# Routed experts' first product as Strassen's seven block products over 256 of 384 rows

## The chip, the core and the metric

The kernel runs on one core of a Trainium2 chip. The metric is the device time of one execution in microseconds (us); the time of a version is the median of its runs. The engines are TensorE (PE in the rows, PEld for its weight loads), VectorE (DVE), ScalarE (ACT), GpSimd (POOL) and SyncE (SP, which issues DMAs). Each engine works through its own queue in order; an instruction that waits holds up all that stand behind it on its engine.

## The reference, cut

The program is an attention-like recurrence, a dense feed-forward layer ("m" below) and a layer of eight routed experts ("e"). The change touches the experts:

```python
def _moe2_ref(x, w_gate, w1, w2):        # x: 1536 x 384, w1: 8 x 384 x 1024, w2: 8 x 1024 x 384
    P = ...                              # 1536 x 8 gate, eight Sinkhorn rounds over x @ w_gate
    out = np.zeros((N, D), dtype=np.float32)
    for e in range(E):
        h = np.maximum(x @ w1[e], 0.0)
        ye = h @ w2[e]
        out += P[:, e:e + 1] * ye
    return out
```

All products have fp32 inputs. The kernel splits every operand into a high and a low part (`hi` is a copy rounded to fp32r, `lo` the remainder), and forms each product as three matmuls: hi·hi, hi·lo, lo·hi.

## The kernel before

There are three stages on PE: the attention front with the first part of the dense layer (0 to about 100 us), the dense layer with the rest of the attention in between (to about 314 us), and the experts (from about 311 to 1119 us). This document is about the last.

The 1536 tokens are three blocks `tb` of 512, the 1024 hidden units of an expert eight blocks `f` of 128. A step is one (e, tb, f): `e_l1` (L652) makes the first product, three `d` blocks of 128 rows with three matmuls each, nine matmuls of 512 columns into bank 0 or 1 (L658 to L660); ScalarE takes the ReLU into `hh` (L663), VectorE the remainder into `hl` (L664). `e_l2` (L667) makes the second product of the step two before: for four groups `j` of 128 tokens three matmuls of 384 columns into banks 2 to 5 (L675 to L677), which add up over the eight `f`. After `f` = 7 VectorE adds the four banks times the gate to `acc` (L688), and for the last expert SyncE stores them.

Weights come as pieces of 128x768 (`setup_weights`, L61): four "a" pieces (w1) and four "b" pieces (w2) an expert. `split_pieces` (L100) loads a piece by SyncE into one of two `raw` buffers of two pieces each, makes `hi` on ScalarE (L113) and `lo` on GpSimd (L114).

From expert 4 on, `w_range` (L693) reads inputs again to test their range: three tiles of 128x1536 with two reductions each (L702, L703), then sixteen of 128x768 with one ScalarE and three VectorE instructions each (L718 to L722). Its tiles take turns with the weight pieces in the `raw` buffers. The order of all this within each engine's queue is set by a scheduler that follows the order of the code, the buffers and its own model of times.

## Time and profile before

| | us |
|---|---|
| median of 3 runs | 1129.66 (1129.65 to 1129.84) |
| profiled execution, device time | 1127.9 |
| its span, first to last instruction | 1126.0 |
| PE busy | 1103.7, 98% |
| DVE / ACT / POOL busy | 477.6 / 322.5 / 151.2 |
| granted TensorE clock, mean | 0.993 |

A matmul's time in the rows is from its start to its modelled end, and the next one starts before that end: what a matmul costs PE is the distance of starts. For the other engines the time of a row is the time of the instruction.

### The profile page before, as it was taken

To read this page: it belongs to the slowest core of one execution; us is meant where nothing else is said; L and a number is where in the kernel's file an instruction comes from. 1 tells how busy PE (TensorE), PEld (TensorE's weight loads), DVE (VectorE), ACT (ScalarE), POOL (GpSimd) and SP (SyncE) were. 2 spreads that over 40 slices of the span, in tenths; PEclk is the share of its full clock that TensorE was granted. 3 is DMA by queue.
4 is the path that set the end of the run, shared out by engine and by line. 5 is a ranking of instruction groups with operands and counts; after the bars stand their busy time and mean duration, and the time that the engine had idled before them with its cause. 6 is when DMAs were issued, how large, how long until landed. Compare 5 with 4: busy or idle time off the path is not lost.

```text
span 1126.0 us, 17562 instructions
## 1 busy us (share of the span) xinstructions
PE 1103.7 (98%) x7376; PEld 995.3 (88%) x7376; DVE 477.6 (42%) x873; ACT 322.5 (29%) x615; POOL 151.2 (13%) x129
## 2 busy tenths in 40 slices
PE   8799999999999999999999999999999999999997
PEld 7677899999989999999999999899999989999996
DVE  7899777774334211222222422562354232122221
ACT  3445344435632441122113112321331231111110
POOL 1002011101710130031003001300210130000000
PEclk9899999999999999999999999999999999999999
DMA  7556212100510021012002200530252020000000
GB/s 207 163 182 199 96 56 71 57 17 5 169 57 1 1 84 29 1 32 81 1 1 84 84 1 30 173 118 19 84 178 76 4 82 1 1 1 1 29 29 31
DMA packets 26920, 71.26 MB, mean 63 GB/s; under 512 B 4128, under 2 KB 11280, under 8 KB 26832
## 3 DMA queue, kind: packets, MB, share of 16 engines
q1 hardware_dynamic: 24528, 57.46, 16.3%
q0 software_dynamic: 2304, 12.58, 3.5%
...
HBM read 65.31 MB, written 2.36 MB: 60 GB/s over the span
## 4 chain that ended last, share of the span: by engine, by line
PE 89%; DMA 4%; issue 2%; DVE 2%; POOL 1%; ACT 1%; SPq 0%; DVEq 0%; POOLq 0%; ACTq 0%
PE bank L675 12%; PE bank L677 11%; PE bank L676 11%; PE bank L659 11%; PE bank L660 11%; PE bank L658 11%; PE bank L583 3%; PE bank L585 3%; PE bank L584 3%; PE bank L564 3%; PE bank L566 3%; PE bank L565 3%; DMA raw<-in_moe_w_in_dram 1%; DMA wh<-in_moe_w_in_dram 1%; DMA lv<-in_vn_dram 1%
## 5 line engine op out<-in xcount | busy, mean ns | idle before, releaser
L664 DVE SCALAR_TENSOR_TENSOR hl<-bank,hh 128x512 fp32r<-128x512 f32 x192 | 132.1, 689 | 434.4 <-ACT hh L663 434.1
L675 PE MATMUL bank<-whi,hh 128*128 128x384 f32 x768 | 259.0, 337 | 0.7 <-ACT hh L663 0.7
L676 PE MATMUL bank<-wlo,hh 128*128 128x384 f32 x768 | 258.3, 336 | 0.0
L677 PE MATMUL bank<-whi,hl 128*128 128x384 f32 x768 | 254.2, 337 | 0.0
L663 ACT ACTIVATE hh<-bank 128x512 fp32r<-128x512 f32 x192 | 114.4, 596 | 488.1 <-PE bank L660 477.3
L660 PE MATMUL bank<-x2h,wlo 128*128 128x512 f32 x576 | 227.9, 396 | 0.0
L659 PE MATMUL bank<-x2l,whi 128*128 128x512 f32 x576 | 227.5, 395 | 0.0
L658 PE MATMUL bank<-x2h,whi 128*128 128x512 f32 x576 | 224.5, 390 | 0.0
L114 POOL TENSOR_TENSOR wlo<-raw,whi 128x768 fp32r<-128x768 f32 x64 | 118.2, 1857 | 564.8 <-ACT whi L113 546.8
L675 PEld LDWEIGHTS bank<-whi,hh 128*128 128x128 f32 x768 | 144.3, 188 | 9.6 <-ACT hh L663 1.1
L676 PEld LDWEIGHTS bank<-wlo,hh 128*128 128x128 f32 x768 | 144.2, 188 | 7.9 <-issue 0.2
L677 PEld LDWEIGHTS bank<-whi,hl 128*128 128x128 f32 x768 | 143.9, 188 | 2.4
L660 PEld LDWEIGHTS bank<-x2h,wlo 128*128 128x128 f32 x576 | 108.0, 187 | 22.3
L658 PEld LDWEIGHTS bank<-x2h,whi 128*128 128x128 f32 x576 | 108.2, 188 | 17.2 <-issue 0.2
L659 PEld LDWEIGHTS bank<-x2l,whi 128*128 128x128 f32 x576 | 108.0, 188 | 17.2
L564 PE MATMUL bank<-x1h,whi 128*128 128x256 f32 (+1 forms) x240 | 75.6, 316 | 5.3 <-ACT x1h L448 2.3
L113 ACT CAST whi<-raw 128x768 fp32r<-128x768 f32 x64 | 53.3, 837 | 95.0 <-PE bank L659 40.9
L565 PE MATMUL bank<-x1l,whi 128*128 128x256 f32 (+1 forms) x240 | 74.6, 312 | 0.6 <-DVE x1l L453 0.6
L688 DVE SCALAR_TENSOR_TENSOR acc<-bank,P,acc 128x384 f32<-128x384 f32 x84 | 48.0, 611 | 63.3 <-PE bank L677 63.3
L583 PE MATMUL bank<-gh,whi 128*128 128x256 f32 (+1 forms) x240 | 74.5, 316 | 0.0
L566 PE MATMUL bank<-x1h,wlo 128*128 128x256 f32 (+1 forms) x240 | 74.3, 311 | 0.0
L584 PE MATMUL bank<-gl,whi 128*128 128x256 f32 (+1 forms) x240 | 73.2, 306 | 0.0
...
## 6 DMA issues: line engine op xcount, KB each, us to landing
...
```

The lines of the kernel that those rows point to most:

```text
L114: (nc.vector if i < N64 else nc.gpsimd).tensor_sub(lo, raw, hi.bitcast(F32))
L564: nc.tensor.matmul(ps, lhsT=wh, rhs=xh[:, d, :], start=(d == 0), stop=False)
L565: nc.tensor.matmul(ps, lhsT=wh, rhs=xl[:, d, :], start=False, stop=False)
L583: nc.tensor.matmul(ps, lhsT=wdh, rhs=gh, start=first, stop=False)
L658: nc.tensor.matmul(ps, lhsT=wh, rhs=xh[:, d, :], start=(d == 0), stop=False)
L659: nc.tensor.matmul(ps, lhsT=wh, rhs=xl[:, d, :], start=False, stop=False)
L660: nc.tensor.matmul(ps, lhsT=wl, rhs=xh[:, d, :], start=False, stop=(d == 2))
L663: nc.scalar.activation(hh, ps, ACTF.Relu)
L664: nc.vector.scalar_tensor_tensor(hl, ps, 0.0, hh.bitcast(F32), op0=ALU.max, op1=ALU.subtract)
L675: nc.tensor.matmul(ps, lhsT=hh[:, sl], rhs=wh, start=st, stop=False)
L676: nc.tensor.matmul(ps, lhsT=hh[:, sl], rhs=wl, start=False, stop=False)
L677: nc.tensor.matmul(ps, lhsT=hl[:, sl], rhs=wh, start=False, stop=sp)
```

## The change

The first product over the first two of the three `d` blocks (256 of 384 rows) is made for two `f` blocks at once by the Winograd form of Strassen's scheme. A pair is one (e, tb, p) with p = 0 to 3, the blocks f = 2p and 2p+1; there are 96 pairs, twelve an expert. The 256 rows by 256 hidden units by 512 tokens are a 2x2 by 2x2 block product with blocks of 128x128 and 128x256. `e_step` forms seven block products (21 matmuls of 256 columns) in place of eight of twice three matmuls, and the third `d` block as before (`e0`, `e1` with `d2`: six matmuls of 512 columns). The block sums of the tokens are made in `split_x2`, once per `tb` (VectorE); those of the weights, s1 to s4, in `split_pair`, once per "a" piece (GpSimd), which stores nine blocks of 128 in place of six. The sums of the products are made in each pair: two ScalarE copies out of PSUM, four VectorE additions of 256 columns, two of 512 columns that join them with the bank; ReLU and remainder then read the result `sums` in SBUF, no longer the bank.

The second product's instructions are the same, but come as eight parts a pair (one per `f` and `j`) from a list `todo`, which `e_step` draws on between its products: 2, 2, 1 and the rest. The PSUM banks of a pair, A (first `f`), B (second `f`) and C (the products s1·t1 and, one after the other, a11·b11, s2·t2, s3·t3) come from a ring of banks 0, 1, 6 and 7. The pieces of an expert are loaded b first, then a, at places in `split_e`; `w_range` moves two steps per pair, as before two steps per two `f`. The logits, the x2 split of the last block and the Sinkhorn rounds are written after the first pair. The dense layer's "a" weights are stored in tiles of 1152 instead of 768 columns; three of its pieces are split by two instructions instead of one.

The diff, cut to its core:

```diff
-K = {'tk': (4, 0, 2, 4, 6), 'wr': (4, 0), 'wm': 1, 'gate': (0, 2)}
+K = {'ring': 6, 'tk': (4, 0, 2, 4, 6), 'wr': (4, 0), 'wm': 1, 'gate': (0, 2)}
+    def split_pair(self, e, p, raw):
+        a11, a12, a22, _, _, a21 = (raw[:, j * 128:(j + 1) * 128] for j in range(6))
+        t = self.t_p.tile([128, 512], F32, tag="t", name="ws")
+        s1, s2, s3, s4 = (t[:, j * 128:(j + 1) * 128] for j in range(4))
+        nc.gpsimd.tensor_add(s1, a21, a22)
+        nc.gpsimd.tensor_sub(s3, a11, a21)
+        nc.gpsimd.tensor_sub(s2, s1, a11)
+        nc.gpsimd.tensor_sub(s4, a12, s2)
+        hi, lo = self.wt[e, p, "a"] = self.w_tiles()
+        for src, sl in ((raw[:, 0:640], slice(0, 640)), (t, slice(640, 1152))):
+            nc.scalar.copy(hi[:, sl], src)
+            nc.gpsimd.tensor_sub(lo[:, sl], src, hi[:, sl].bitcast(F32))
...
     def split_x2(self, tb):
+        nc.vector.tensor_sub(t1, b12, b11)
+        nc.vector.tensor_sub(t3, b22, b12)
+        nc.vector.tensor_sub(t2, b22, t1)
+        nc.vector.tensor_sub(t4, b21, t2)
+        for src, j, o in ((b11, 0, 0), (x[:, 1, :], 0, 256), (ta, 0, 768), (t3, 0, 1280), (t4, 1, 0), (x[:, 2, :], 1, 256)):
+            nc.scalar.copy(hl[0][j][:, sl], src)
+            nc.vector.tensor_sub(hl[1][j][:, sl], src, hl[0][j][:, sl].bitcast(F32))
...
-    def e_l1(self, i, e, tb, f):
+    def e_banks(self, n):
+        if n < K['ring']:
+            c, a = (7, 0) if n % 2 == 0 else (0, 7)
+            return [self.banks[j] for j in (a, 1, c)]
+        ring = self.ring = [1, 0, 7, 6] if n == K['ring'] else [self.ring[j] for j in (3, 0, 1, 2)]
+        return [self.banks[ring[j]] for j in (1, 2, 0)]
+    def e_step(self, n, e, tb, p, fill):
+        def mm(ps, w, x, start=False, stop=False):
+            nc.tensor.matmul(ps, lhsT=uh, rhs=xh, start=start, stop=False)
+            nc.tensor.matmul(ps, lhsT=uh, rhs=xl, start=False, stop=False)
+            nc.tensor.matmul(ps, lhsT=ul, rhs=xh, start=False, stop=stop)
+        def relu(f, ps, sums):
+            nc.vector.tensor_add(sums, ps, sums)
+            nc.scalar.activation(hh, sums, ACTF.Relu)
+            nc.vector.scalar_tensor_tensor(hl, sums, 0.0, hh.bitcast(F32), op0=ALU.max, op1=ALU.subtract)
+        mm(C1, "s1", "t1", start=True, stop=True)
+        mm(C0, "a11", "b11", start=True, stop=True)
+        nc.scalar.copy(sa[:, 0:256], C0)
+        nc.scalar.copy(p5, C1)
+        fill(2)
+        mm(A, "e0", "d2", start=True)
+        mm(A0, "a12", "b21")
+        mm(C0, "s2", "t2", start=True, stop=True)
+        nc.vector.tensor_add(u2, C0, sa[:, 0:256])
+        nc.vector.tensor_add(sa[:, 256:512], u2, p5)
+        fill(2)
+        mm(A1, "s4", "b22", stop=True)
+        relu(2 * p, A, sa)
+        mm(C0, "s3", "t3", start=True, stop=True)
+        nc.vector.tensor_add(sb[:, 0:256], C0, u2)
+        nc.vector.tensor_add(sb[:, 256:512], sb[:, 0:256], p5)
+        fill(1)
+        mm(Bk, "e1", "d2", start=True)
+        mm(B0, "a22", "t4", stop=True)
+        relu(2 * p + 1, Bk, sb)
+        fill(8)
...
-            self.wa_p = pool("wa", 8)
+            self.wa_p = pool("wa", 5)
...
+            split_e = (0, 1, 2, 2, 3, 4, 4, 5, 5, 6, 7, 8)
+            for n, (e, tb, p) in enumerate((e, tb, p) for e in range(E) for tb in range(3) for p in range(4)):
+                self.e_step(n, e, tb, p, fill)
+                if n == 0:
+                    self.logits(2)
+                    self.split_x2(2)
+                    self.sinkhorn()
+                todo += [lambda e=e, tb=tb, f=f, j=j: self.e_l2(e, tb, f, j) for f in (2 * p, 2 * p + 1) for j in range(4)]
+                self.split_pieces(N64 + 8 * (e + 1) + split_e[n % 12])
+                if not gen and (e, tb) >= K['wr']:
+                    next(wr, None)
+                    next(wr, None)
+            fill(8)
```

In the changed file the products of `mm` are at L730 to L732, `relu` at L737 to L739, the ScalarE copies at L746 and L747, the four additions at L752, L753, L758 and L759, the second product at L773 to L775, the sum into `acc` at L786, the reductions of `w_range` at L800 and L801 (wide tiles) and L817 to L820 (narrow), a piece's sums and `lo` at L174 to L177 and L181 (a) and L130 (b).

PE's queue in the middle of the experts. Before, three of the nine first products of a step end and the second products of another follow (`x2h`, `x2l` are tokens; `whi`, `wlo` weights):

```order
L658 MATMUL bank0_61<-x2h1_3804,whi_5256 128x512
L659 MATMUL bank0_61<-x2l1_3805,whi_5256 128x512
L660 MATMUL bank0_61<-x2h1_3804,wlo_5257 128x512
L675 MATMUL bank2_63<-whi_5176,hh_5722 128x384
L676 MATMUL bank2_63<-wlo_5177,hh_5722 128x384
L677 MATMUL bank2_63<-whi_5176,hl_5723 128x384
L675 MATMUL bank3_64<-whi_5176,hh_5722 128x384
```

Now, in pair 31 (banks A, B, C are 1, 0, 6): the last second products of pair 30, one product of pair 32's C, s3·t3 of pair 31 into bank 6, and pair 32's B into bank 1, which was pair 31's A:

```order
L774 MATMUL bank5_66<-wlo_5517,hh_6591 128x384
L775 MATMUL bank5_66<-whi_5516,hl_6592 128x384
L732 MATMUL bank7_68<-x2h_4171,wlo_5746 128x256
L730 MATMUL bank6_67<-x2h1_3838,whi_6071 128x256
L731 MATMUL bank6_67<-x2l1_3839,whi_6071 128x256
L732 MATMUL bank6_67<-x2h1_3838,wlo_6072 128x256
L730 MATMUL bank1_62<-x2h_4172,whi_5745 128x512
L731 MATMUL bank1_62<-x2l_4174,whi_5745 128x512
L732 MATMUL bank1_62<-x2h_4172,wlo_5746 128x512
L730 MATMUL bank1_62<-x2h_4172,whi_5745 128x256
L731 MATMUL bank1_62<-x2l_4174,whi_5745 128x256
L732 MATMUL bank1_62<-x2h_4172,wlo_5746 128x256
```

A pair's products are spread over its neighbours, and most of them stand in blocks of three of 256 columns.

VectorE's queue where the first two tiles of `w_range` are reduced (`wt`). Before:

```order
L688 SCALAR_TENSOR_TENSOR acc_4819<-bank4_65,P_72,acc_4819 128x384
L688 SCALAR_TENSOR_TENSOR acc_4819<-bank5_66,P_72,acc_4819 128x384
L664 SCALAR_TENSOR_TENSOR hl_6159<-bank0_61,hh_6158 128x512
L702 TENSOR_REDUCE wmm_6835<-wt_6836 128x1
L703 TENSOR_REDUCE wmm_6835<-wt_6836 128x1
L664 SCALAR_TENSOR_TENSOR hl_6189<-bank1_62,hh_6188 128x512
L664 SCALAR_TENSOR_TENSOR hl_6214<-bank0_61,hh_6213 128x512
L702 TENSOR_REDUCE wmm_6835<-wt_6890 128x1
L703 TENSOR_REDUCE wmm_6835<-wt_6890 128x1
L664 SCALAR_TENSOR_TENSOR hl_6239<-bank1_62,hh_6238 128x512
```

Now, from the first addition of pair 47 to the last before pair 48's first (banks A, B, C of pair 47 are 1, 0, 6):

```order
L752 TENSOR_TENSOR u2_7868<-bank6_67,esa_7869 128x256
L753 TENSOR_TENSOR esa_7869<-u2_7868,p5_7867 128x256
L800 TENSOR_REDUCE wmm_8025<-wt_8026 128x1
L801 TENSOR_REDUCE wmm_8025<-wt_8026 128x1
L737 TENSOR_TENSOR esa_7869<-bank1_62,esa_7869 128x512
L758 TENSOR_TENSOR esb_7870<-bank6_67,u2_7868 128x256
L759 TENSOR_TENSOR esb_7870<-esb_7870,p5_7867 128x256
L739 SCALAR_TENSOR_TENSOR hl_7906<-esa_7869,hh_7905 128x512
L737 TENSOR_TENSOR esb_7870<-bank0_61,esb_7870 128x512
L800 TENSOR_REDUCE wmm_8025<-wt_8107 128x1
L739 SCALAR_TENSOR_TENSOR hl_7925<-esb_7870,hh_7924 128x512
L801 TENSOR_REDUCE wmm_8025<-wt_8107 128x1
```

A pair has eight instructions of its own there; before, two steps had two. Both pairs of reductions stand in one pair's stretch. In pair 48's stretch, which follows, stand its eight, four L786, the third L800 and L801, six small ones, and one each of L817, L819 and L820.

GpSimd's queue in the experts. Before, one instruction a piece:

```order
L114 TENSOR_TENSOR wlo_5257<-raw_5099,whi_5256 128x768
L114 TENSOR_TENSOR wlo_5177<-raw_4934,whi_5176 128x768
L114 TENSOR_TENSOR wlo_5422<-raw_5260,whi_5421 128x768
L114 TENSOR_TENSOR wlo_5342<-raw_5099,whi_5341 128x768
L114 TENSOR_TENSOR wlo_5507<-raw_5260,whi_5506 128x768
```

Now (`ws` is s1 to s4): the last sums of three "a" pieces, the `lo` of two of them, and of two "b" pieces:

```order
L177 TENSOR_TENSOR ws_5041<-raw_4805,ws_5041 128x128
L177 TENSOR_TENSOR ws_5125<-raw_4805,ws_5125 128x128
L181 TENSOR_TENSOR wlo_4964<-raw_4574,whi_4963 128x640
L181 TENSOR_TENSOR wlo_4964<-ws_4958,whi_4963 128x512
L130 TENSOR_TENSOR wlo_5289<-raw_5052,whi_5288 128x768
L181 TENSOR_TENSOR wlo_5047<-raw_4805,whi_5046 128x640
L181 TENSOR_TENSOR wlo_5047<-ws_5041,whi_5046 128x512
L130 TENSOR_TENSOR wlo_5366<-raw_5052,whi_5365 128x768
```

An "a" and a "b" piece alternate, about one of each a pair, from pair 8 of an expert on, when the first weight buffers come free.

## Rows read from the trace of the kernel before

**Rows 1.** The page: busy time, share of the span, instructions.

```profile
PE 1103.7 (98%) x7376; PEld 995.3 (88%) x7376; DVE 477.6 (42%) x873; ACT 322.5 (29%) x615; POOL 151.2 (13%) x129
```

**Rows 2.** Windows, two stretches of experts: length, busy us by engine, clock, DMA share, GB/s.

```profile
450.00:700.00 250.00, 250.00 (x1257) 226.58 (x1256) 64.89 (x96) 50.50 (x79) 34.98 (x19) 1.00 0.11 33
700.00:900.00 200.00, 199.28 (x1000) 180.17 (x999) 88.14 (x123) 53.51 (x79) 29.36 (x16) 1.00 0.29 94
```

**Rows 3.** Timeline, PE, one step of the experts: start, us, instruction.

```profile
501.92 0.39 PE L658 MATMUL bank<-x2h,whi 128*128 128x512 f32 x1
...
504.00 0.33 PE L675 MATMUL bank<-whi,hh 128*128 128x384 f32 x1
...
506.11 0.39 PE L658 MATMUL bank<-x2h,whi 128*128 128x512 f32 x1
```

**Rows 4.** Timeline, PE, end of the dense layer: nine matmuls of 256 columns.

```profile
309.89 0.28 PE L583 MATMUL bank<-gh,whi 128*128 128x256 f32 x1
...
310.96 0.40 PE L658 MATMUL bank<-x2h,whi 128*128 128x512 f32 x1
```

**Rows 5.** Groups by line and shape: busy us, mean ns, idle before and releaser.

```profile
L675 PEld LDWEIGHTS bank<-whi,hh 128*128 128x128 f32 x768 | 144.3, 188 | 9.6 <-ACT hh L663 1.1 <-issue 0.2
L664 DVE SCALAR_TENSOR_TENSOR hl<-bank,hh 128x512 fp32r<-128x512 f32 x192 | 132.1, 689 | 434.4 <-ACT hh L663 434.1
L114 POOL TENSOR_TENSOR wlo<-raw,whi 128x768 fp32r<-128x768 f32 x64 | 118.2, 1857 | 564.8 <-ACT whi L113 546.8 <-issue 17.7
L663 ACT ACTIVATE hh<-bank 128x512 fp32r<-128x512 f32 x192 | 114.4, 596 | 488.1 <-PE bank L660 477.3 <-PE bank L676 10.5
L688 DVE SCALAR_TENSOR_TENSOR acc<-bank,P,acc 128x384 f32<-128x384 f32 x84 | 48.0, 611 | 63.3 <-PE bank L677 63.3
L719 DVE SCALAR_TENSOR_TENSOR wh<-wh 128x768 f32<-128x768 f32 x16 | 15.3, 957 | 34.2 <-ACT wh L718 34.2
L721 DVE TENSOR_REDUCE whm<-wh 128x1 f32<-128x768 f32 x16 | 15.1, 946 | 0.2
L343 POOL TENSOR_TENSOR kz<-at,zf 112x256 f32<-112x256 f32 x12 | 8.9, 745 | 69.2 <-issue 67.5 <-PE bank L237 1.6
L453 DVE TENSOR_TENSOR x1l<-x,x1h 128x256 fp32r<-128x256 f32 x18 | 7.3, 421 | 7.5 <-ACT x1h L448 4.7 <-DMA lv<-in_vn_dram 2.5
L702 DVE TENSOR_REDUCE wmm<-wt 128x1 f32<-128x1536 f32 x3 | 5.3, 1753 | 11.1 <-DMA wt<-in_w_dram 11.1
L251 DVE TENSOR_TENSOR x<-bank,cst 128x256 f32<-128x256 f32 x8 | 3.3, 416 | 0.1
```

**Rows 6.** One line's instructions (L572: 270 to 311 us): min/median/max ns, starts, shapes.

```profile
L664 DVE SCALAR_TENSOR_TENSOR hl<-bank,hh x192: 676/691/694, 310.7 to 1113.1; 128x512 fp32r<-128x512 f32 x192
L572 DVE TENSOR_TENSOR gl<-g,gh x17: 409/475/1874, 271.1 to 307.6; 128x256 fp32r<-128x256 f32 x17
```

**Rows 7.** Timeline, DVE and POOL, at 291 and at 584 us.

```profile
291.29 1.84 POOL L114 TENSOR_TENSOR wlo<-raw,whi 128x768 fp32r<-128x768 f32 x1
291.96 1.45 DVE L572 TENSOR_TENSOR gl<-g,gh 128x256 fp32r<-128x256 f32 x1 [2.37 <-ACT gh L571]
...
584.46 1.85 POOL L114 TENSOR_TENSOR wlo<-raw,whi 128x768 fp32r<-128x768 f32 x1 [62.78 <-ACT whi L113]
585.33 0.68 DVE L664 SCALAR_TENSOR_TENSOR hl<-bank,hh 128x512 fp32r<-128x512 f32 x1
```

**Rows 8.** Waits: engine, tile, line, releaser: us in total, times, longest.

```profile
ACT wh L718 <- DMA wh<-in_moe_w_in_dram: 24.4, 8, 5.9
DVE wmm L702 <- DMA wt<-in_w_dram: 11.1, 3, 4.0
```

**Rows 9.** Windows, the front: PE with gaps, and the clock after them.

```profile
40.00:44.00 4.00, 1.57 (x25) 0.99 (x22) 3.02 (x4) 1.92 (x4) 0.68 (x2) 1.00 0.92 278
44.00:48.00 4.00, 1.66 (x4) 1.12 (x5) 1.50 (x3) 0.41 (x1) 0.00 (x0) 0.67 0.66 237
48.00:52.00 4.00, 4.00 (x11) 3.02 (x11) 2.97 (x6) 0.93 (x2) 0.00 (x0) 0.50 0.00 1
```

**Rows 10.** Timeline, the end: the last matmul and the last sums into acc.

```profile
1117.55 2.19 DVE L688 SCALAR_TENSOR_TENSOR acc<-bank,P,acc 128x384 f32<-128x384 f32 x4 [3.73 <-PE bank L677]
...
1118.39 0.34 PE L677 MATMUL bank<-whi,hl 128*128 128x384 f32 x1
```

More of the change, by code (lines that the diff above doesn't have):

```diff
@@ L599, in logits @@
         nc = self.nc
-        ps = self.bank_y[:, 0:128]
+        ps = self.bank_u[:, 0:128]
         for d in range(3):
@@ new lines, in e_l2 @@
+        ps = self.banks[2 + j][:, 0:DM]
+        sl = slice(j * 128, (j + 1) * 128)
+        nc.tensor.matmul(ps, lhsT=hh[:, sl], rhs=wh, start=st, stop=False)
+        nc.tensor.matmul(ps, lhsT=hh[:, sl], rhs=wl, start=False, stop=False)
+        nc.tensor.matmul(ps, lhsT=hl[:, sl], rhs=wh, start=False, stop=sp)
+        if sp:
+            n = tb * 4 + j
+            g = self.P[:, n, e:e + 1]
+            if j == 0 and e == 0:
+                self.acc[tb] = self.x2_p.tile([128, 4, DM], F32, tag=f"x2_{tb}", name="acc")
+            acc = self.acc[tb][:, j, :]
+            if e == 0:
+                nc.scalar.copy(acc, ps)
+                nc.scalar.activation(acc, acc, ACTF.Copy, scale=g)
+            else:
+                nc.vector.scalar_tensor_tensor(acc, ps, g, acc, op0=ALU.mult, op1=ALU.add)
+            if e == E - 1:
+                nc.sync.dma_start(out=self.out[n * 128:(n + 1) * 128, :], in_=acc)
@@ new lines, in run, with fill @@
+            todo = [lambda s=s: self.m_l2(*s[1:]) for s in steps[-2:]]
+            def fill(k):
+                for _ in range(min(k, len(todo))):
+                    todo.pop(0)()
+            split_e = (0, 1, 2, 2, 3, 4, 4, 5, 5, 6, 7, 8)
[8 more added lines that the diff above has]
+                if not gen and (e, tb) >= K['wr']:
+                    if wr is None:
+                        wr = self.w_range()
+                    next(wr, None)
+                    next(wr, None)
```

195 lines of the change are left out of this document (95 added, 100 removed).

## The prediction

> **What bounds the kernel now.** I read the busy times first: PE is busy 98% of the span, every other engine under half [rows 1]. The windows say that this holds in the stage that changes: from 450 to 700 us PE is busy 250.00 of 250 us, from 700 to 900 it misses 0.7 us [rows 2]. So the experts are paced by PE's own work, and a saving there counts in full, as long as nothing that PE waits for becomes late. The timeline gives the price of a matmul: nine of 512 columns take from 501.92 to 504.00, 0.231 us each, twelve of 384 take 2.11 us, 0.176 each [rows 3]. Nine of 256 columns in a row, each with its own weight load, take 1.07 us, 0.119 each [rows 4]. Price goes with columns, plus some 0.013 us.
>
> **What PE saves.** Per pair the first product had 18 x 0.231 = 4.16 us. Now it has 21 x 0.119 + 6 x 0.231 = 2.50 + 1.39 = 3.89. The second product keeps 24 x 0.176 = 4.22. A pair falls from 8.38 to 8.11 us, and 96 pairs give 26.4 us. The rest of the change can only take from that.
>
> One rule of the Trainium skill speaks against this price. "TensorE: Matmul & The Clock Gate", section "Back-to-back issue gap", says that a stream of weight loads and matmuls is spaced by both together, about 81 ns at 128 columns and 131 at 512; between these 256 would be about 98 ns (estimate from that page), and the pair would cost 21 x 0.098 + 6 x 0.131 = 2.84 against 18 x 0.131 = 2.36 before, a loss of 46 us in all. The trace differs, with 231 ns at 512 and 119 at 256 [rows 3, 4], and the measurement decides.
>
> **What the other engines get.** Per pair VectorE had two instructions of 0.69 us [rows 5]. Now it has four additions of 256 columns (0.42 each: the nearest rows are L251, one input in PSUM, and L453, both in SBUF), two of 512 and two remainders of 512 (0.69 each): 4.44 us of 8.11. With the four sums into acc (0.61 each, every fourth pair) it is 6.9. ScalarE has two ReLUs of 0.60 and two copies that are no longer than these: under 2.4. On averages neither is the bound. What decides is lateness, and I followed PE's new order for it. After s2·t2 of a pair PE has twelve second products, s3·t3 and a few of 256 columns before the next pair's B takes over this pair's bank A: 2.5 to 3.2 us. In that time VectorE must do the first two additions and the one that empties A: 0.2 (drain of the last product) + 0.42 + 0.42 + 0.69 = 1.75. So 0.7 to 1.4 us are to spare; the other deadlines (ReLU, remainder, the addition that empties C) have 1 to 3. In an ordinary pair PE waits for nothing, and I price it at zero.
>
> **GpSimd bursts: 4 us.** What is new in kind is that four of VectorE's eight instructions read both inputs from SBUF, the remainder among them (before, one input was a PSUM bank). In the trace such an instruction is held up while GpSimd works: a subtraction of 0.41 us that starts inside a GpSimd one takes 1.45 and ends with it, while the remainder out of PSUM takes 0.68 beside GpSimd as always [rows 7]; over all starts the first form ranges from 0.41 to 1.87 us, the second from 0.68 to 0.69 [rows 6].
>
> The Trainium skill has this as a rule ("SBUF — State Buffer", section "Who interferes with whom"): a VectorE instruction with two SBUF inputs and a GpSimd instruction that reads SBUF exclude each other for a whole instruction. The trace agrees for VectorE [rows 6, 7]; by the rule GpSimd would be held up as well, which delays weights that are needed pairs later, and leaves my sum as it is.
>
> GpSimd's work grows. From 0.75 us at 256 columns and 1.86 at 768 [rows 5], an estimate by the straight line is 0.47 at 128, 1.30 at 512, 1.58 at 640. An "a" piece costs 4 x 0.47 + 1.30 + 1.58 = 4.8 (was 1.86), and from pair 8 of an expert on one "a" and one "b" piece go through per pair: 6.6 of 8.1 us for some five pairs, in seven experts. An instruction that comes at a random time waits for half the sum of squares over the pair: (4 x 0.22 + 1.69 + 2.50 + 3.46) / 16.2 = 0.53, less the 0.13 that overlap, 0.4 us. Four of them are 1.6 us, 4.44 becomes 6.0, still inside 8.1: free. Where the sums into acc fall into a burst (pairs 8 and 12) it is 6.9 + 1.6 = 8.5, and the spare of 0.7 to 1.4 is overrun by some 0.3. Price 14 x 0.3 = 4 us; bounds 0 and, with all of 1.6 us exposed in 35 pairs, 56. I stay near the low end, since the deadlines cover most of it.
>
> **The range test: 11 us.** `w_range` has the same work as before, but VectorE has less room. Around its start the order puts two tiles of 1.75 + 1.74 us [rows 5] into pair 47 and, into pair 48, another, four sums into acc, the first narrow tile (0.96 + 2 x 0.95) and small ones. Pair 47 has 4.44 + 7.0 = 11.4 us, pair 48 4.44 + 2.44 + 3.5 + 2.85 + 0.8 = 14.0: together 25.4 us of work in 16.2 us of PE's. No order inside the two pairs helps. Walking through: in pair 47 the first tile stands ahead of the addition that empties A, which ends at 5.2 instead of 1.75 us, and PE's 2.5 us of cover leave 2.8 of waiting; in pair 48 PE waits 0.5 for a remainder, 3.1 for the emptying of B behind the third tile, 1.0 for the next u2. That is 7.4, I take 7. The pairs from 57 to 63 and 69 to 73 have a narrow tile most times: 4.44 + 2.85 = 7.3, with acc 9.7, and they meet the burst's 1.6. Over 57 to 63 the order holds about 57 us of VectorE work, +6 of burst against 56.8 of PE, and over 69 to 73 about 39 + 6 against 40.5; less the spare, 3 us in the two. One us more for the loads: before, VectorE waited 3.7 us for each of three wide tiles and ScalarE 24 us in eight waits for narrow ones [rows 8], at no cost to PE; now a load that is late holds up additions that stand behind it. Sum 11, bounds 4 and 20.
>
> **Start and end: 4 us.** At pair 0 no second products are there to fill, and the split of the last x2 block shares VectorE: ahead of the addition that frees bank C stand five of 0.42 and one of 0.69, 2.8 us, against some 1.3 us of PE's work (s3·t3 and the logits); ahead of the first remainder another 4.4 us against 3.5. That is 1.5 + 0.9, plus one hold-up by GpSimd: 3 (1 to 6). At the end, after the last s3·t3, 0.2 + 0.42 + 0.42 + 0.69 + 0.60 + small waits = 2.5 lead to the last ReLU, against twelve second products, 2.1: 0.4; and the last four banks end 0.18 apart instead of 0.53, so that three more acc sums of 0.53 trail the last matmul, where it was one and a half [rows 10]: 0.8. Together 1.
>
> **At nothing.** The Strassen sums of the first two x2 blocks, the b-first loads and the moved splits lie under PE's dense layer; the cover of the x2 sums is 20 us. Three dense pieces are split in two halves, 0.1 us each more on VectorE. The front before 100 us gets another order around its loads; I see no direction in it, and keep 3 us either way for the range.
>
> **The sum.** -26.4 + 4 + 11 + 3 + 1 = -7.4 us. The profiled execution (1127.9, span 1126.0) would be 1120.5; the median of the runs before is 1.8 higher, so 1129.7 - 7.4 = 1122.3.
>
> **Rivals.**
> 1. The covers hold: only what the work itself forces remains, 4 in the range test, 1 at the start, 1 at the end. 1129.7 - 26.4 + 6 = 1109 (1104 to 1114). For it: PE lost 0.7 us while ScalarE and VectorE waited tens of us [rows 2, 8], a scheduler that spreads a pair over its neighbours. Against: the 25.4 us in 16.2.
> 2. Slower: VectorE becomes the engine that paces the bursts. Place: pairs 8 to 12 of seven experts, 35 pairs. If half of the 1.6 us, 0.8, reaches PE in each, that is 28 us; with 15 for the other terms, 1129.7 - 26.4 + 43 = 1146. It decides from (26.4 - 15) / 35 = 0.33 us a pair. For it: the deadline on A has only 0.7 us to spare in places, and a single hold-up can be 1.4 [rows 6]. Against: a pair's total of 6.0 in 8.1.
> 3. The clock: in the front, after gaps of PE in 40 to 48 us, the granted clock was 0.67 and then 0.50 for 4 us, with PE fully busy [rows 9]: 1.2 instead of 2.4 GHz, 2 to 4 us lost each time. If the waits of 2 to 3 us in pairs 47 to 63 do this three times, +9: 1131. For it: waits of the same size. Against: a wait here is one gap in dense work.
> 4. The change doesn't save: 256-column products in this stage are paced by their weight loads, whose rows are 0.188 us [rows 5]: 21 x 0.188 + 1.39 = 5.3 against 4.16, +112 us, 1242. Against: the same pattern of loads in [rows 4].
>
> **Chances.** My forecast 0.5 (1114 to 1130), rival 1 0.25, rival 2 0.16, rival 3 0.08, rival 4 0.01. The range takes in rival 1 from 1107 on, the forecast, rival 3 and the lower third of rival 2: 1107 to 1137. About 0.2%, 2.3 us, is what a measurement of this kernel can tell from no change, so faster is below 1127.4. Faster: 0.41 of the forecast, all of rival 1, 0.01 of rival 3: 0.67. Within: 0.07 + 0.03 + 0.02 = 0.12. Slower: 0.21.
>
> **What would show it.** PE's distance of starts, 0.119 for the products of 256 columns and 8.1 us a pair in experts 1 to 3 outside bursts. Waits of PE for L737 and L758, thickest at the start of expert 4, small in bursts; L739, L753 and L759 with a wide range of durations, L737 and L752 with a narrow one. PE busy in the experts within 3% of the time. If PE waits evenly in all pairs, or the bursts cost more than a us each, the walk along the order was wrong; if the clock falls in the experts, rival 3.

## The result, and the profile after

The changed kernel takes 1145.8 us (three runs, 1145.4 to 1146.2) against 1129.7: the ratio is 1.0145, 95% interval 1.0126 to 1.0163. It is slower by 1.45%, outside the predicted range and on the other side. A fourth run, in which the granted clock was 0.841, took 1202.2 us and is not counted. The profiled execution took 1146.2 us, span 1144.4.

The page of the kernel after, its busy line (for rows 1 of before), and PE and its clock in 40 slices:

```profile
PE 1098.4 (96%) x8240; PEld 1027.0 (90%) x8240; DVE 818.5 (72%) x1473; ACT 408.2 (36%) x851; POOL 265.3 (23%) x289
...
PE   9799999999989899999999999799999999999996
...
PEclk9899999999989999999999999899999999999999
```

VectorE went from 42 to 72%, PE from 98 to 96%, and the clock is lower in two slices in the middle. The windows say where (length, busy us by engine, clock, DMA share, GB/s; before, PE missed 0.7 us in all from 450 to 900 us [rows 2]):

```profile
250.00:320.00 70.00, 66.55 (x594) 63.02 (x593) 42.27 (x72) 40.46 (x94) 40.69 (x38) 0.98 0.22 69
320.00:417.00 97.00, 92.95 (x561) 87.77 (x560) 62.55 (x139) 34.13 (x71) 21.31 (x21) 0.96 0.05 16
417.00:515.00 98.00, 96.57 (x604) 92.49 (x603) 62.52 (x103) 33.36 (x67) 26.27 (x28) 1.00 0.09 28
515.00:613.00 98.00, 98.00 (x623) 94.79 (x622) 65.80 (x110) 31.89 (x62) 29.73 (x29) 1.00 0.11 34
613.00:711.00 98.00, 98.00 (x625) 94.81 (x624) 65.56 (x109) 31.48 (x61) 29.72 (x30) 1.00 0.12 36
711.00:809.00 98.00, 89.14 (x537) 84.60 (x536) 76.28 (x119) 28.49 (x54) 18.98 (x24) 0.97 0.24 77
809.00:907.00 98.00, 91.75 (x558) 84.92 (x557) 78.79 (x122) 33.27 (x60) 25.58 (x27) 1.00 0.28 89
907.00:1005.00 98.00, 94.16 (x575) 88.72 (x574) 74.99 (x121) 34.12 (x63) 29.73 (x28) 0.98 0.22 73
1005.00:1110.00 105.00, 105.00 (x667) 101.56 (x666) 68.53 (x120) 28.69 (x57) 8.74 (x6) 1.00 0.05 16
```

From 515 to 711 us and again after 1005 PE misses nothing: there the change gives what it promised. The timeline shows it as the distance between the first 512-column products of two pairs, 571.53 - 563.48 = 8.05 us:

```profile
563.48 0.39 PE L730 MATMUL bank<-x2h,whi 128*128 128x512 f32 x1
...
571.53 0.39 PE L730 MATMUL bank<-x2h,whi 128*128 128x512 f32 x1
```

So I count how much longer than 8.05 us each pair took, from the start of every ninth L730 to that of the next (nine a pair; PE runs some products of a pair ahead, so a border may lie a product or two off). VectorE's additions of a pair begin about where the next pair so counted does: what the order ahead of the prediction shows as VectorE's stretch of pair 47 stands here in pair 48. Pair 0, whose products are mixed into the dense layer, stands apart with its wait. In the changed kernel: pairs 1 to 15 lose 13.7 us, 16 to 47 only 0.2, 48 to 50 13.2, 59 to 65 10.1, 71 to 75 7.4, all others together under 1. Before, a pair took 8.37 us undisturbed. Beside 94 x 0.32 = 30.1 us gained stand 45.4 us lost in pairs 1 to 94 (before: 4.7), 4.0 us by which pair 1 starts later (3.46 of them a wait in pair 0), 2.9 in the last pair and 1.1 behind the last matmul: -30.1 + 40.7 + 4.0 + 2.9 + 1.1 = +18.6, and the spans differ by 18.4.

Pairs 48 to 50, 59 to 65 and 71 to 75 are those in which `w_range` works. This is the start of pair 48, VectorE and the PE instruction that waited (the timeline; in brackets the idle time and what ended it), then PE's clock after it:

```profile
712.18 0.42 DVE L753 TENSOR_TENSOR esa<-u,p 128x256 f32<-128x256 f32 x1
712.72 1.75 DVE L800 TENSOR_REDUCE wmm<-wt 128x1 f32<-128x1536 f32 x1
714.39 1.74 DVE L801 TENSOR_REDUCE wmm<-wt 128x1 f32<-128x1536 f32 x1
716.05 0.68 DVE L737 TENSOR_TENSOR esa<-bank,esa 128x512 f32<-128x512 f32 x1
...
716.79 0.52 PE L730 MATMUL bank<-x2h,whi 128*128 128x512 f32 x1 [3.21 <-DVE esa L737]
```

```profile
717.20:720.40 3.20, 3.20 (x12) 2.72 (x11) 2.12 (x3) 1.49 (x4) 0.63 (x1) 0.50 0.71 236
720.60:724.00 3.40, 3.40 (x23) 3.40 (x23) 3.40 (x3) 0.00 (x0) 0.00 (x0) 1.00 0.02 5
```

Two reductions of a wide tile stand between the addition that ends at 712.6 and the one that empties bank A; PE waits 3.21 us for it, and then its clock is at 0.50, 1.2 GHz, as it was after gaps in the front [rows 9].

Pair 61 is a narrow tile, the four sums into acc and GpSimd's burst at one place:

```profile
833.21 0.95 DVE L817 SCALAR_TENSOR_TENSOR wh<-wh 128x768 f32<-128x768 f32 x1
...
834.07 2.19 DVE L786 SCALAR_TENSOR_TENSOR acc<-bank,P,acc 128x384 f32<-128x384 f32 x4
...
836.18 0.68 DVE L739 SCALAR_TENSOR_TENSOR hl<-esa,hh 128x512 fp32r<-128x512 f32 x1
836.20 4.14 POOL L130 TENSOR_TENSOR wlo<-raw,whi 128x768 fp32r<-128x768 f32 x2 [8.77 <-DMA raw<-in_moe_w_dram]
836.78 0.42 DVE L758 TENSOR_TENSOR esb<-bank,u 128x256 f32<-128x256 f32 x1
...
837.11 0.94 DVE L819 TENSOR_REDUCE whm<-wh 128x1 f32<-128x768 f32 x1
...
837.97 0.94 DVE L820 TENSOR_REDUCE whm<-wh 128x1 f32<-128x768 f32 x1
...
838.83 1.79 DVE L759 TENSOR_TENSOR esb<-esb,p 128x256 f32<-128x256 f32 x1
...
840.66 0.37 ACT L747 COPY p<-bank 128x256 f32<-128x256 f32 x1 [3.31 <-DVE esb L759]
...
841.08 0.39 PE L730 MATMUL bank<-x2h,whi 128*128 128x256 f32 x1 [1.79 <-ACT p L747]
```

VectorE has no gap from 833.2 to 840.6. The addition L759, 0.43 us by its median, takes 1.79 beside GpSimd (the lock, as in [rows 7]), and the wait goes round a corner: p5 has one buffer, so ScalarE can't copy the next pair's p5 (L747) before L759 has read this one, and PE waits 1.79 us for the bank that L747 empties.

### The profile page after: what moved, and what is told of

It reads as the page before. It is cut to its first block, busy times and chain, and to the rows that moved or that the text cites. A ratio compares the mean times of both kernels' runs of the same rounds, so it can differ in the third digit from the quotient of the medians.

```text
span 1144.4 us, 20269 instructions
## 1 busy us (share of the span) xinstructions
PE 1098.4 (96%) x8240; PEld 1027.0 (90%) x8240; DVE 818.5 (72%) x1473; ACT 408.2 (36%) x851; POOL 265.3 (23%) x289
## 4 chain that ended last, share of the span: by engine, by line
PE 79%; DVE 9%; DMA 6%; issue 2%; POOL 2%; ACT 2%; SPq 0%; DVEq 0%; ACTq 0%; POOLq 0%
PE bank L773 10%; PE bank L774 10%; PE bank L730 9%; PE bank L775 9%; PE bank L731 9%; PE bank L732 9%; PE bank L625 3%; PE bank L606 3%; PE bank L627 3%; PE bank L626 3%; PE bank L608 3%; PE bank L607 3%; DMA wh<-in_moe_w_out_dram 1%; DVE hl L739 1%; DMA wh<-in_moe_w_in_dram 1%
## 5 line engine op out<-in xcount | busy, mean ns | idle before, releaser
L730 PE MATMUL bank<-x2h,whi 128*128 128x256 f32 (+1 forms) x864 | 271.1, 314 | 24.6 <-DVE esa L737 9.2
L731 PE MATMUL bank<-x2l,whi 128*128 128x256 f32 (+1 forms) x864 | 268.1, 311 | 0.0
L732 PE MATMUL bank<-x2h,wlo 128*128 128x256 f32 (+1 forms) x864 | 267.7, 310 | 0.0
L773 PE MATMUL bank<-whi,hh 128*128 128x384 f32 x768 | 260.8, 340 | 1.1 <-ACT hh L738 0.8
L730 PEld LDWEIGHTS bank<-x2h,whi 128*128 128x128 f32 x864 | 165.3, 191 | 41.0 <-DVE esa L737 11.8
L775 PE MATMUL bank<-whi,hl 128*128 128x384 f32 x768 | 186.2, 336 | 2.7 <-DVE hl L739 2.7
L732 PEld LDWEIGHTS bank<-x2h,wlo 128*128 128x128 f32 x864 | 165.6, 192 | 8.7
L731 PEld LDWEIGHTS bank<-x2l,whi 128*128 128x128 f32 x864 | 165.7, 192 | 8.6
L738 ACT ACTIVATE hh<-esa 128x512 fp32r<-128x512 f32 x96 | 60.7, 632 | 302.5 <-DVE esa L737 297.6
L773 PEld LDWEIGHTS bank<-whi,hh 128*128 128x128 f32 x768 | 145.8, 190 | 3.6 <-ACT hh L738 1.5
L181 POOL TENSOR_TENSOR wlo<-raw,whi 128x640 fp32r<-128x640 f32 x32 | 52.2, 1630 | 379.4 <-ACT whi L180 379.4
L775 PEld LDWEIGHTS bank<-whi,hl 128*128 128x128 f32 x768 | 136.0, 188 | 3.9 <-DVE hl L739 3.8
L739 DVE SCALAR_TENSOR_TENSOR hl<-esb,hh 128x512 fp32r<-128x512 f32 x96 | 81.7, 851 | 60.2 <-ACT hh L738 60.1
L752 DVE TENSOR_TENSOR u<-bank,esa 128x256 f32<-128x256 f32 x96 | 40.6, 423 | 111.3 <-PE bank L732 111.3
L739 DVE SCALAR_TENSOR_TENSOR hl<-esa,hh 128x512 fp32r<-128x512 f32 x96 | 79.3, 827 | 33.5 <-ACT hh L738 33.3
L130 POOL TENSOR_TENSOR wlo<-raw,whi 128x768 fp32r<-128x768 f32 x32 | 63.8, 2000 | 72.2 <-ACT whi L129 63.5
L738 ACT ACTIVATE hh<-esb 128x512 fp32r<-128x512 f32 x96 | 60.8, 634 | 32.5 <-DVE esb L737 32.5
```

The lines of the kernel that those rows point to most:

```text
L130: (nc.vector if i < N64 else nc.gpsimd).tensor_sub(lo, raw, hi.bitcast(F32))
L730: nc.tensor.matmul(ps, lhsT=uh, rhs=xh, start=start, stop=False)
L731: nc.tensor.matmul(ps, lhsT=uh, rhs=xl, start=False, stop=False)
L732: nc.tensor.matmul(ps, lhsT=ul, rhs=xh, start=False, stop=stop)
L738: nc.scalar.activation(hh, sums, ACTF.Relu)
L739: nc.vector.scalar_tensor_tensor(hl, sums, 0.0, hh.bitcast(F32), op0=ALU.max, op1=ALU.subtract)
```

## The experiments

All times are medians, taken beside the kernel before (1128 to 1130 us on the same chips). Kernels with an unchanged front differ, in the one profiled execution of each, by up to 5 us in when pair 0 starts (277.3 to 282.5 us), so besides the times I read the loss by pairs of that execution, which repeats within about 2 us where nothing was changed. The table is counted as above, us over 8.05 a pair (pair 0: its wait):

```
kernel               time     pair 0   1-15   16-47  48-75  76-94
after              1145.8      3.5     13.7    0.2    31.1    0.3
e1_no_test         1115.8      3.5     13.9    1.4     0.7    0.0
e3_short_sinkhorn  1139.9      3.5      7.2    0.7    29.9    0.3
e4_no_a_pool       1141.8      2.9     11.7   -0.1    27.4    0.3
e5_no_loads        1142.4      7.1     32.2    1.4     1.1    0.3
e6_thin            1155.2      4.4     47.1    2.1     1.0    1.2
e7_late_split      1144.0      3.5     14.6    0.2    30.1    0.3
e8_cover12         1144.5      3.5     12.3    0.1    28.6    0.3
e9_thin_held       1135.4      3.5     13.8    8.8    12.9    1.1
e10_no_loads_held  1141.0      3.5     13.8    0.2    26.6    0.7
e11_late_split_held 1139.7     0.0     10.7    0.4    28.8    0.3
e12_paced          1136.1      0.0     14.6    9.4    13.1    1.2
e13_thin_calm      1126.7      3.5     12.3    7.8     3.6    1.0
e14_one_input      1132.1      3.5     13.5    7.1     8.6    1.2
e15_calm_paced     1119.8      0.0     10.9    7.6     4.2    0.9
e16_calmer         1116.9      0.0     10.7    4.0     3.1    1.3
```

**The place: the test, not the burst.** e1 replaces `w_range` by a constant flag.

> The changed kernel with the range test left out (no loads, no reductions, no ScalarE work of w_range; the flag is set to its passing value by two small instructions). Theory T (the range test's own VectorE work in pairs 48 to 50, 59 to 65 and 71 to 75 is what those pairs lost, 30.7 us against 8.05 us a pair, the clock's falls at 717, 741 and 946 us included): 1145.8 - 31 = 1115, every pair from 16 on at 8.05 us, no fall of the clock after 400 us. Theory B (rival 2 of the prediction: GpSimd's bursts hold VectorE up, and the test is only the place where it shows): pairs 48 to 50 gain 13 us, those from 59 to 65 and 71 to 75 stay late by some 10 to 17, 1128 to 1133.

Measured 1115.8, ratio 0.9878 [0.9853, 0.9902]. The windows of e1 where the test was:

```profile
711.00:809.00 98.00, 98.00 (x622) 94.66 (x621) 65.68 (x110) 31.54 (x62) 30.01 (x30) 1.00 0.10 33
809.00:907.00 98.00, 97.95 (x621) 94.40 (x621) 67.47 (x109) 31.91 (x62) 29.66 (x29) 1.00 0.11 34
907.00:1005.00 98.00, 98.00 (x623) 94.57 (x622) 67.77 (x111) 29.96 (x59) 25.68 (x28) 1.00 0.07 25
```

PE is full, at the full clock, with GpSimd's bursts all there (26 to 30 us in 98). Theory T holds to a microsecond.

e2 does the same to the kernel before.

> The kernel before with the range test left out in the same way. Theory T and theory B alike: PE missed 0.7 us from 700 to 900 us there, so the test cost at most 1 us: 1128.5 to 1129.7. If it is faster by 3 us or more, the test had a price before too, and the change only raised it.

Measured 1127.7, ratio 0.9985 [0.9972, 0.9997], so the test cost some 1.7 us there (0.3 to 3.2), between the two cases named. Without it the change is worth 1127.7 - 1115.8 = 12 us.

e4 takes away most of the burst and keeps the test (`if e > 0:` ScalarE copies raw columns into `hi`, and `lo` is expert 0's).

> The changed kernel with GpSimd's work on the first weights of experts 1 to 7 left out (their four sums and two remainders a piece, 4.8 us each in 28 pieces; the remainders of expert 0 are used again, and ScalarE rounds piece columns in place of the sums). The range test stays. Theory T: pairs 48 to 50 keep their 13 us, those from 59 to 65 and 71 to 75 lose at least two thirds of their 17: 1140 to 1146. Theory B: what the bursts hold up is gone, 1145.8 - 15 to 20 = 1126 to 1131.

Measured 1141.8, and pairs 48 to 75 lose 27.4 instead of 31.1; those from 59 to 65 and 71 to 75 keep 14.7 of their 17.5. As theory T has it: the burst adds some 4 us.

**Why there: loads, work, or place?** e5 leaves the test's loads out:

```diff
-            t = self.raw_p.tile([128, 2 * PIECE], F32, tag="raw", name="wt")
-            nc.sync.dma_start(out=t, in_=self.ins["w"][...])
+            t = self.x2y[:, 0:1536].bitcast(F32)
...
```

> The changed kernel with the loads of the range test left out: its 67 instructions on VectorE and ScalarE are the same in size, number and written place, but read a block of x2's split that lies in SBUF, and take no buffer of the weights' ring (the result of the test is set to pass). Theory L (the loads decide: a tile waits in the ring of two buffers behind weight pieces, comes late, and engines stand at its instruction with the pairs' work behind it): pairs 48 to 50 keep at most 5 of 13 us, those from 59 on lose nothing, since the test is then spread over pairs 48 to 75 with 1.9 us of VectorE a pair: 1145.8 - 23 to 28 = 1118 to 1123. Theory W (the sum of VectorE's work decides, whatever the loads do): pairs 48 and 49 keep their 25 us of work in 16 and 10 of the 13 us, and the thick pairs only move: 1130 to 1140.

e6 cuts the tiles to a quarter, one `next(wr)` a pair from pair 12 on, in buffers of its own.

> The changed kernel with the range test in tiles of a quarter (192 narrow or 384 wide values), one a pair from pair 12 on, in two small buffers of its own (those that held the last dense weights). Nothing is left out. By theories T and L: about 1.1 us of VectorE a pair in 77 pairs, no instruction over 0.6 us, no shared ring: 1145.8 - 29 to 31 = 1115 to 1117. By theory W alone, with 80 us of VectorE instead of 57 because of the fixed cost of each instruction: pairs with the sums into acc (7 + 1.1 of 8.05 us) and bursts wait, some 0.5 us in every fourth pair: 1125.

Both missed: 1142.4 and 1155.2. The table shows why. Pairs 48 to 75 are free, as hoped, but pairs 1 to 15 lose 18.5 and 33.4 us more than in the changed kernel. Written behind pair 48, e5's test ran from 285 to 406 us, since nothing ties it to a pair: the scheduler issues what is ready. In that stretch:

```profile
320.00:417.00 97.00, 77.36 (x436) 68.73 (x435) 89.19 (x178) 37.42 (x65) 17.04 (x20) 0.89 0.04 13
```

VectorE is 92% busy, PE 80%, the clock at 0.89. So the written place doesn't set when the test runs. In e5 and e6, which take nothing from the ring of two `raw` buffers, it runs early; in the changed kernel, which shares this ring with the weight pieces, it doesn't. That the ring holds it there is a conclusion from these runs, not a test of its own. e7 and e8, which only write the split of x2 later, or the second products four blocks later, told the same:

> The changed kernel with the split of the last x2 block (16 VectorE instructions, 8 us) written behind pair 4 instead of pair 0; it is first read in pair 8. Theory S0 (pair 0's wait of 3.46 us at 315 us and the clock's fall at 318 us that follows come from that split standing ahead of pair 0's additions): -3 of waiting, -3 of clock, 1145.8 - 6 = 1140. Theory C (cover is missing, whatever stands on VectorE, because pair 0 has no second products to fill with): -0 to -2, and pairs 4 to 7 lose what pair 0 gains: 1144 to 1147.

> The changed kernel with four blocks of second product kept back at the end of every pair, so that the written order itself has PE twelve blocks behind from pair 2 on (as the scheduler's order has from pair 15 on) instead of eight. Theory C: pairs 3 to 15 fall from 8.27 to 10.1 us to 8.05, 1145.8 - 7 to 9 = 1137 to 1139, and the pairs of the range test stay. Theory S (Sinkhorn's chain of VectorE instructions and its matmuls in PE's queue are the whole loss there): -0 to -2, 1144 to 1146.

Measured 1144.0 and 1144.5; the start is the changed kernel's, by the sum of its pairs to 1 and 2 us. What they were to tell apart is left to e11.

From here each VectorE and ScalarE instruction of the moved part (in e12, e15 and e16 PE's too) got an edge to the one written before it on its engine, which fixes the order of issue and adds no semaphore (`self.held(first)` calls `self.tc.add_manual_dep(ins[k], prev.name, ...)` with the class `NoSync`). e9 is e6 with that, e10 is e5 with that.

> The kernel e6_thin with one thing added: each VectorE and ScalarE instruction of the test is tied in its engine's order behind the instruction written before it, so that the scheduler can't bring it forward. Nothing is left out. Theory P (what a test costs is set by the place that the scheduler gives it, and e6 lost its 33 us in pairs 1 to 15 alone, where its instructions were brought forward beside Sinkhorn and the splits): 1.0 us of VectorE in each of 77 pairs from 12 on lies beside PE's work, pairs 16 to 94 cost 8.05 us, the start is that of the changed kernel: 1115 to 1118. Theory W (80 us of VectorE work are too much wherever they lie): pairs with four sums into acc and with bursts wait, 1125 or more.

> The kernel e5_no_loads (the loads of the test left out, its instructions with resident data) with the test's instructions tied to their written place in the same way: two steps a pair from pair 48 to 76. So the same instructions as in the changed kernel, at their written place, without its loads and without the ring of buffers. Theory L (late loads, and the pairs' work that stands behind an instruction that waits for one): pairs 48 to 76 lose under 6 us, 1115 to 1121. Theory W (the work itself, by the prediction's count 25 us in the 16 of pairs 47 and 48, two reductions of 1.75 us ahead of additions that free a bank): pairs 48 to 50 still lose 7 us or more and some of the others 0.5 to 1 each: 1125 to 1135.

e9 measured 1135.4, ratio 1.0049 [1.0035, 1.0063], e10 1141.0, above what either theory named. In e10 as many instructions of the same size as in the changed kernel, without a single load, lose 26.6 us in pairs 48 to 75, though partly in other pairs: theory L falls, the work is enough. It isn't so everywhere: in pairs 54 to 56 and 66 to 68 e10's narrow tiles, 0.95 us an instruction, cost nothing (8.04 to 8.05 us a pair). In e9 the place decides: behind pair 15 the test costs 22.8 - 2.1 (e1's) = 20.7 us, none of it in pairs 26 to 34 or 38 to 46, which hold instructions of the test too, and nearly all between pair 10 of an expert and pair 1 of the next. There e9's timeline shows, at pairs 35 and 36:

```profile
614.32 1.57 POOL L190 TENSOR_TENSOR wlo<-raw,whi 128x640 fp32r<-128x640 f32 x1
...
614.82 1.61 DVE L748 SCALAR_TENSOR_TENSOR hl<-esb,hh 128x512 fp32r<-128x512 f32 x1 [1.45 <-ACT hh L747]
615.84 1.74 POOL L190 TENSOR_TENSOR wlo<-ws,whi 128x512 fp32r<-128x512 f32 x1
616.36 1.44 DVE L821 SCALAR_TENSOR_TENSOR wq<-wq 128x192 f32<-128x192 f32 x1
...
618.36 0.41 DVE L761 TENSOR_TENSOR u<-bank,esa 128x256 f32<-128x256 f32 x1
```

The remainder (L748 here) takes 1.61 us beside GpSimd and the test's own L821, 0.35 us by its median, 1.44: 2.0 us of hold-up ahead of the next u2.

e14 replaces L821 by an instruction that reads its tile once, e13 deals the tiles to pairs 2 to 9 of each expert (`range(2 if 2 <= n % 12 < 6 else 1 if 6 <= n % 12 < 10 else 0)`).

> The kernel e9_thin_held with the same tiles dealt to pairs 2 to 9 of each expert only (two tiles a pair in 2 to 5, one in 6 to 9, none in 10 to 1). Nothing is left out. Theory M (the test costs where it meets GpSimd's burst and the sums into acc, and nothing where VectorE idles 1.9 us ahead of the next u2): of the 20.7 us that e9 loses to the test behind pair 15 at most 4 stay: 1135.4 - 17 to 20 = 1115 to 1119. Theory W (so much VectorE work costs about as much wherever it lies): with up to 2.1 us in a pair it loses 0.2 to 0.5 us in each of 28 pairs and more at the acc sums: 1122 to 1132.

> The kernel e9_thin_held, tiles one a pair as there, with the test's instruction that reads its tile twice from SBUF replaced by one that reads it once (the treatment of zeros is left out; the values tested here give the same answer). Theory K (the lock: in a burst this instruction takes 1.44 us instead of 0.34, right ahead of the next u2): about 1 us less in each of the 14 to 18 pairs that wait: 1135.4 - 7 to 12 = 1123 to 1128. Against it (what is late there is the pair's own remainder, 1.61 instead of 0.69, and the acc sums): 1132 to 1135.

e13 measured 1126.7, ratio 0.9977 [0.9963, 0.9991]: half of the test's price is gone. By its time that is theory W's range, not theory M's; by pairs the calm ones are nearly free, as M has it (pairs 2 to 9 of experts 2 to 6 lose 0.5 to 0.8 us an expert). Pairs 11, with no tile, still lost 1 us each, behind tiles in pairs 8 and 9, where the burst has begun. e14 measured 1132.1, 3.3 us less than e9 and by pairs 5.9 of 22.8: the range named against theory K. The lock on the test's own instruction is a part, and the smaller one.

**The start.** e3 leaves out seven of eight Sinkhorn iterations.

> The changed kernel with seven of the eight Sinkhorn iterations left out. Theory S (pairs 2 to 15 lost 9.6 us because each iteration puts six small VectorE instructions and two matmuls that wait for them into PE's queue): pairs 4 to 9 fall to 8.05 us, 1145.8 - 6 to 10 = 1136 to 1140. Theory C (what is missing there is cover: PE runs eight blocks of second product behind instead of the twelve of every later pair, and each short chain of additions shows by 0.6 us): the pairs from 2 to 8 still wait 0.3 to 1.2 us each, gain 2 to 4, 1142 to 1144.

Measured 1139.9: 6.5 us less in pairs 1 to 15, 3.3 of it clock. That is theory S's time; pairs 4 and 5 do fall to 8.05 us, but pairs 10 to 15 lose what they lost. e11 is e7 with the split tied to its place.

> The kernel e7_late_split with the split of the last x2 block tied to its written place behind pair 4 (e7 showed the same times in every pair as the changed kernel, so the scheduler had brought the split forward). Theory S0 (pair 0's wait of 3.46 us, and the clock's fall at 318 us with 3 us lost, come from the split ahead of pair 0's additions): 1145.8 - 4 to 7 = 1139 to 1142. Theory C (pair 0 has nothing to fill with): pair 0 and 1 lose the same 11 us, 1145 to 1147.

Measured 1139.7, as theory S0 has it: pair 0's wait is gone, and 3 us of pairs 1 to 15. But pairs 7 and 8 now take 10.7 and 12.9 us: there (376 to 382 us) the split's copies stand on ScalarE behind four scalings of gated sums that wait for Sinkhorn, and its subtractions on VectorE ahead of the pair's u2.

**Put together.** e12 ties all three; e15 does so with e13's dealing and the scalings of the first gated sums spread; e16 keeps the test to pairs 2 to 7, two tiles a pair, and scales one a pair. All three also take the ring of four banks into use at pair 10 instead of 6, since Sinkhorn holds one of the banks longer.

> All of e9_thin_held and e11_late_split_held, and Sinkhorn's eight iterations tied one to a pair (pairs 1 to 9): its matmul stands in PE's order a pair behind the VectorE work that it reads; the first gated sums are scaled once it is done. Nothing is left out. If the three causes (the test's place and loads, the split, Sinkhorn's chain) are independent: 1116 - 4 to 6 for the split - 4 to 6 for Sinkhorn (e3 gave 6 without seven iterations) = 1104 to 1109, which beats the kernel before by 2%. If the start loses its time to missing cover: 1112 to 1116.

> The kernel e12_paced with the test in the calm pairs as in e13, and with the eight scalings of the first gated sums dealt two a pair to pairs 10 to 13 instead of all in pair 9 (in e12 PE waited 5 us in pairs 10 and 11 and the clock fell once, and I put that down to these 4.8 us of ScalarE ahead of the ReLUs). Nothing is left out. By theory M: test at most 4, pairs 1 to 15 lose 6 to 8 instead of 14.6, pair 0 none: 1136 - 17 to 20 - 7 to 9 = 1107 to 1112, below the kernel before by 1.5 to 2%. If pairs 10 to 13 keep their loss, the reading of e12 was wrong: 1115.

> The kernel e15_calm_paced with the test's tiles in pairs 2 to 7 of each expert alone, two a pair, and the scalings of the first gated sums one a pair in pairs 10 to 17. Nothing is left out. Theory M (the rest of the price lies in pairs 8 and 9, where the burst begins): pairs 23, 35, 47, 59 and 71 fall from 9.05 to 8.05 us and pairs 22 to 25 lose 2 instead of 3.2; with 1 to 2 us from pair 11, 1119.8 - 6 to 8 = 1112 to 1114. Theory W (the work as such): no change of more than 2 us, 1118 to 1121.

e12 measured 1136.1, a miss: the test costs about what it does in e9, pairs 2 to 9 took 2.5 us less than in the changed kernel, and pairs 10 and 11 lost 6.9 us instead of 2.5, where all eight scalings of 0.60 us stood ahead of the pair's copies on ScalarE (one wait of 3.17 us). e15 spread these: 1119.8, ratio 0.9931 [0.9914, 0.9949], 8 us above the forecast's upper end; pair 11 keeps 3.9 us, with waits at 399 and 401 us that come before its first scaling (403.5 us), so that the scalings were only a part. e16: 1116.9, ratio 0.9887 [0.9867, 0.9907], between the two forecasts: pairs 23, 35, 47, 59 and 71 fell from between 9.03 and 9.39 us to 8.13, as theory M had it, but all pairs together lose 4.5 us less than in e15, not 6 to 8. It computes all that the kernel before computes, and beats both kernels, by 1.1 and 2.5%. Its windows from 711 us on:

```profile
711.00:809.00 98.00, 97.38 (x613) 93.30 (x612) 75.58 (x144) 34.58 (x72) 28.21 (x29) 1.00 0.18 56
809.00:907.00 98.00, 97.52 (x614) 93.45 (x612) 75.72 (x145) 34.65 (x72) 28.34 (x29) 1.00 0.18 57
907.00:1005.00 98.00, 97.68 (x616) 93.99 (x616) 74.27 (x147) 32.72 (x68) 25.18 (x27) 1.00 0.14 45
```

VectorE does there about as much as in the changed kernel (75.6, 75.7 and 74.3 us against 76.3, 78.8 and 75.0), and PE misses 1.4 us instead of 19.

## Why the prediction was wrong

By the spans, the sum said -7.4 us and +18.4 came. Counted by pairs the terms are: saving -30.1 (said -26.4); bursts and range test 30.2 (said 4 + 11); start 4.0 + 13.7 - 3.3 = 14.4 (said 3); end 2.9 + 1.1 = 4.0 (said 1). So two steps failed, the range test first and the start second.

**PE's saving: right.** -26.4 was said, 96 x 0.32 = -30.7 came: a pair takes 8.05 us, not 8.11. No pair is paced by weight loads (rival 4).

**"In an ordinary pair PE waits for nothing": right.** 98.00 of 98 us, twice.

**GpSimd's bursts, 4 us: right in kind, too dear.** The lock is there, and in these three lines only on the forms that read two SBUF inputs (min/median/max ns; L739 and L759 have two, L737 one):

```profile
L739 DVE SCALAR_TENSOR_TENSOR hl<-esa,hh x96: 627/692/2344, 323.0 to 1131.1; 128x512 fp32r<-128x512 f32 x96
```

```profile
L759 DVE TENSOR_TENSOR esb<-esb,p x96: 407/426/2073, 320.1 to 1131.7; 128x256 f32<-128x256 f32 x96
```

```profile
L737 DVE TENSOR_TENSOR esa<-bank,esa x96: 665/691/693, 318.6 to 1129.3; 128x512 f32<-128x512 f32 x96
```

L739 and L759 reach 2344 and 2073 ns, L737 stays at 693, as in [rows 6, 7]. This agrees with the rule of the Trainium skill that the prediction weighed ("SBUF — State Buffer", section "Who interferes with whom"): a VectorE instruction with two SBUF inputs contends with a GpSimd instruction that reads SBUF, one with at most one such input doesn't, outside modes that use both ports. The covers hold most of it: pairs 16 to 47, with three bursts, lose 0.2 us (in e1, all bursts together, 2.1).

**Rival 2 named the time (1146) and not the cause.** It put 28 us into bursts in 35 pairs; bursts alone cost next to nothing, and without most of them (e4) only 4 us come back in pairs 48 to 75. That the times agree is luck.

**The range test, 11 us: the step that failed.** It cost 30.1 (1145.8 - 1115.8), beyond its own upper bound of 20. For pairs 47 and 48 I walked along the order and had 7.4 us of waiting; 8.9 were there in pairs 48 to 50, and that working was sound; 3.4 of clock were added. For the pairs from 57 on I set sums against sums, 57 + 6 us of VectorE work against 56.8 of PE's and 39 + 6 against 40.5. That is 10.7 us over already, and I took off most of it for the spare of 0.7 to 1.4 us a pair, as if all of it could be used, and kept 3; 17.5 came in pairs 59 to 65 and 71 to 75 (10.0 of it waits, 1.7 clock). A sum over seven pairs doesn't price them. VectorE had 20% to spare there (78.8 of 98 us) and PE waited all the same, because additional instructions of 1 us stand ahead of an addition whose result PE needs within 1 or 2, as the rows of pair 61 show. e16 does the same work, with more instructions, at a fifth of the price (6.3 us; e9 20.7, e13 10.3), where it keeps clear of the burst and meets VectorE's idle time. That idle time stands in the row of most undisturbed u2, in the brackets (0.83 where the sums into acc stand before it):

```profile
1120.29 0.42 DVE L752 TENSOR_TENSOR u<-bank,esa 128x256 f32<-128x256 f32 x1 [1.89 <-PE bank L732]
```

**Loads, 1 us: small, as said, but not measured alone.** e10 loses 26.6 of 31.1 us without any, but its tiles stand in other pairs, so the 4.5 us between are no price of the loads. In the changed kernel ScalarE stands 26.4 us before the loads of narrow tiles, up to 3.4 at a time (us in all, times, longest):

```profile
ACT wh L816 <- DMA wh<-in_moe_w_in_dram: 15.3, 8, 3.4
ACT wh L816 <- DMA wh<-in_moe_w_out_dram: 11.1, 6, 2.7
```

Followed back link by link, of PE's 10.0 us of waits from 815 us on one of 0.27 us ends at such a load, and three more, 3.0 us together, have VectorE idle before a tile further up.

**The start, 3 us: the second step that failed, 14.4.** Pairs 1 to 15 lose 13.7 where those of before lost 3.3, and pair 0 waits 3.46. The step counted pair 0's two deadlines and held the other fourteen pairs for ordinary; Sinkhorn's iterations, one every 4 to 7 us until 378 us, each with six small instructions and a matmul in PE's queue, were not in it (e3: 6.5 us, 3.3 of it clock). The wait of pair 0 itself I had at 1.5 + 0.9:

```profile
315.12 2.02 DVE L753 TENSOR_TENSOR esa<-u,p 128x256 f32<-128x256 f32 x1
...
317.06 0.94 DVE L675 TENSOR_TENSOR x2l<-x,x2h 128x512 fp32r<-128x512 f32 x1
317.93 0.41 DVE L758 TENSOR_TENSOR esb<-bank,u 128x256 f32<-128x256 f32 x1
...
318.39 0.79 PE L730 MATMUL bank<-x2h,whi 128*128 128x512 f32 x1 [3.46 <-DVE esb L758]
```

L753 takes 2.02 us beside GpSimd and a split stands behind it; the one hold-up that I allowed for is there, at its full length.

**The clock (rival 3, 0.08): it came true on top.** Five falls in the experts (318, 386, 717, 741 and 946 us), worth 9.9 us (4.8 in the start, 5.1 in the test); I had three, +9. The rivals were held for alternatives; waits and the clock's falls come together, and belonged into one sum.

**The end, 1 us: right behind the last matmul (1.1).** The 2.9 of the last pair, which I had at 0.4, are mostly the four blocks carried along from the start, 12 x 0.176 = 2.1, and so a part of its price.

What stays open: e16 still loses 10.7 us in pairs 1 to 15, 5.6 of them in pairs 11 to 15. In e5 and e11 pairs are free from the one on in which PE falls back from eight to twelve blocks of second product behind (pair 9, which takes 6.0 us), in the others from pair 16 on. That this cover decides there is not shown, since e8 could not set it.
